# First token product of two batches by seven products, and five weight blocks rounded in attention: a fused attention and MLP-mixer kernel

## The chip, the core and the metric

The kernel runs on one core of one Trainium2 chip. The metric is the device time of one execution in microseconds (us). The core has a matrix engine (TensorE, PE in the profile; it loads weights as PEld and multiplies), a vector engine (VectorE, DVE), a scalar engine for activations and copies (ScalarE, ACT), GpSimd (POOL) and SyncE (SP), which here only issues transfers (DMA). Each engine works through its own list in order and waits on semaphores. Products land in PSUM[...].

## What is computed

Attention with a hash mask, on 4 batches, 8 heads, 768 tokens and 64 channels a head, feeds one MLP-mixer block: a product over the tokens, then one over the channels.

```python
def _attn_ref(q, k, v, proj):
    q_bits = (np.einsum('bhsd,dk->bhsk', q, proj) > 0)      # 6 bits, likewise k_bits
    ...
    mask = q_bucket[:, :, :, None] == k_bucket[:, :, None, :]
    scores = np.where(mask, scale * np.matmul(q, k.transpose(0, 1, 3, 2)), -1000000000.0)
    ...                                                      # softmax over the keys
    return np.matmul(attn, v)

def _moe_ref(x, w_tok1, w_tok2, w_ch1, w_ch2):               # x: 4 x 768 x 512
    xt = x.transpose(0, 2, 1)
    h = np.maximum(xt @ w_tok1, 0.0) @ w_tok2                # w_tok1 768x256, w_tok2 256x768
    u = x + h.transpose(0, 2, 1)
    h2 = np.maximum(u @ w_ch1, 0.0) @ w_ch2                  # w_ch1 512x1536, w_ch2 1536x512
    return (u + h2)
```

The four weights arrive in double precision. The kernel rounds them to single precision itself, from the two 32-bit words of each number, a block of 128 x 768 at a time.

## The kernel before

Attention goes through 16 pairs of heads, numbered 0 to 15; a pair is done in two halves of 384 queries. TensorE makes the scores (L337), ScalarE their exponentials `e` (L344), VectorE adds these up (`esd`, L371 to L378), TensorE weighs the values (L389) and sums over partitions (L413), VectorE refines the reciprocal (L426, L428) and divides (L438). Twelve blocks of weights are rounded meanwhile, one in each of pairs 0 to 11:

```python
# class Conversion, cut: steps of rounding one block
def fetch(self):
    ...
    raw = self.pool.tile([P, NW, 2], U32, name="raw", tag="raw", bufs=self.bufs)
    nc.sync.dma_start(out=raw..., in_=src)                                     # L169
def begin(self):
    size = self.pool.tile([P, NW], F32, name="size", tag="size", bufs=self.bufs - 1)
    nc.scalar.activation(size, raw[:, :, 1].bitcast(F32), ACT.Abs, scale=EXPONENTS)  # L177
def join(self):
    unit = self.pool.tile([P, NW], F32, name="unit", tag="unit", bufs=1)
    nc.vector.tensor_scalar(unit, size, 3, 0x7F800000, shift, and)             # L187
    nc.vector.tensor_scalar(size, size, 3, None, shift)                        # L191
    nc.vector.scalar_tensor_tensor(unit, raw[:, :, 0], 2.0**-52, unit, ...)    # L195
    nc.vector.tensor_tensor(size, size, unit, op=ALU.add)                      # L196
def end(self):
    nc.vector.scalar_tensor_tensor(to, hi, 0x80000000, size, and, or)          # L206
def turnover(self):
    self.end(); self.fetch()
def one(self):
    self.begin(); self.join(); self.end(); self.fetch()
```

```python
# attention's loop, cut
weights = Conversion(pool, [(w_tok1, W1, 3, (0, NR)), (w_tok2, W2, 1, (0, NJ)), (w_ch1, WC1, 1, (0, NCB))], bufs=2)
        for n in range(len(pairs)):
            halves = [Half(n, half) for half in range(2)]
            if n:
                load_v(n + 1)
            for now in halves:
                now.scores()
                if n == now.half == 0:
                    hashes(1)
                now.add()
                if now.half == 0:
                    now.add_last()
            if before:
                before.sums()
            if 0 < n < len(pairs) - 1:
                hashes(n + 1)
            halves[1].add_last()
            if n == 0:
                load_v(1)
            load_qk(n + 2)
            add_values(n)
            weights.begin()
            if before:
                before.newton()
            weights.join()
            halves[0].weigh()
            if n + 1 == len(pairs):
                before.divide()
                before = Quotients(halves)
                before.sums()
                before.newton()
                weights.turnover()
                halves[1].weigh()
                break
            if before:
                before.divide()
            weights.turnover()
            halves[1].weigh()
            if n and n % 2 == 0:
                bounce(pool.tile([P, 2 * S], F32, name="stage", tag="stage", bufs=1), n - 2)
            if n == 2 * NP:
                fetch(0, x0)
            before = Quotients(halves)
```

`bounce` turns two finished pairs of channels (two VectorE transposes, L233) and stores them to DRAM, from where the token stage fetches each batch as `x` with tokens on the partitions (L245).

In the token stage `mix1` makes the first product, 12 matmuls of 512 columns a batch (6 blocks of 128 tokens for each of 2 blocks of hidden units). `mix2` makes the second product by seven products in place of eight (Strassen's method in Winograd's form: sums of quarters on both sides beforehand, sums of the seven results after) and adds the result to XT in on-chip memory with an accumulating DMA. The eight blocks of the second channel weight (`conversion.one`) are rounded meanwhile, one `job` at a time.

```python
# tokens(), cut
        def mix1(b):
            x = (x0, x1)[b % 2]
            if b and turned:
                turn(b, x, banks)
            r1 = pool.tile([P, NJ, DM], F32, name="r1", tag="r1", bufs=2)
            for j in range(NJ):
                ps = bank("t1")
                for r in range(NR):
                    nc.tensor.matmul(
                        ps, W1[:, r, P * j : P * j + P], x[:, r], start=(r == 0), stop=(r == NR - 1),
                    )                                  # L634
                to = r1[:, j]
                if not turned:
                    to = to.rearrange("p (c g i) -> p g c i", c=NCB, i=32)
                    ps = ps.rearrange("p (g c i) -> p g c i", c=NCB, i=32)
                nc.scalar.activation(to, ps, ACT.Relu)
                job()
        ...
        def mix2(b, m):
            r1, new = R1[b]
            a00, a01, s1, a11 = (
                r1[:, k, P * (2 * m + i) : P * (2 * m + i) + P] for i in range(2) for k in range(2)
            )
            ...
            to = places[(2 * b + m + 1) % 3].rearrange("p (i n t) -> p i n t", i=2, n=2)
            p1, u, p7, p57 = (to[:, i, n] for i in range(2) for n in range(2))
            product(0, a00, b00)                       # product: one matmul, L674
            nc.scalar.copy(p1, ps[0])                  # L679
            product(1, a01, b10)
            product(2, s1, sums[:, 0])
            nc.scalar.copy(p57, ps[2])
            product(3, new[:, 1], b01)
            nc.scalar.copy(p7, ps[3])
            product(0, new[:, 0], sums[:, 1], False)
            nc.scalar.copy(u, ps[0])
            product(2, new[:, 2], b11, False)
            product(3, a11, sums[:, 2], False)
            ...                                        # five VectorE sums, L689 to L693
            nc.gpsimd.dma_start(out=XT[...], in_=to, accum_op=ALU.add)   # L694

        for b in range(B):
            mix1(b)
            if b == 0:
                weight_sums()
            left_sums(b)
            if b:
                mix2(b - 1, 0)
                job()
                mix2(b - 1, 1)
        mix2(B - 1, 0)
        inputs(0, T, 0)
        mix2(B - 1, 1)
        while not turned and jobs:
            job()
```

The channel stage follows (L761 is its matmul). It ends with a product whose four quarters go to the output as they are finished:

```python
# product(), cut
issuer = nc.scalar if j == 6 else nc.sync
...
issuer.dma_start(out=final(0, 0), in_=qs[:, 0])                       # L1173
...
issuer.dma_start(out=final(1, 1), in_=qs[:, 3])                       # L1180
...
for i, a in [(1, ps[2]), (2, ps[3])]:
    nc.vector.tensor_tensor(qs[:, i], a, qs[:, i], op=ALU.add)        # L1184
    issuer.dma_start(out=final(i // 2, i % 2), in_=qs[:, i])          # L1185
```

Of the kernel before, what the change touches and what calls it, by code (L numbers as in the profile page):

```python
# [35 lines left out]
F32 = mybir.dt.float32  # L37
# [11 lines left out]
def kernel(  # L49
# [14 lines left out]
    P = 128  # L64
# [76 lines left out]
    class Conversion:  # L141


        def __init__(self, pool, parts, bufs):
            self.pool, self.bufs = pool, bufs
            self.todo = [
                (w, dst, rows, j, n)
                for w, dst, rows, blocks in parts
                for j in range(*blocks, rows)
                for n in range(0, dst.shape[2], NW // rows)  # L150
            ]
            self.fetched, self.begun, self.ready = [], None, None
            for _ in range(bufs - 1):
                self.fetch()
# [17 lines left out]
        def begin(self):  # L172
            if not self.fetched:
                return
            raw, to, rows = self.fetched.pop(0)
            size = self.pool.tile([P, NW], F32, name="size", tag="size", bufs=self.bufs - 1)
            nc.scalar.activation(size, raw[:, :, 1].bitcast(F32), ACT.Abs, scale=EXPONENTS)  # L177
            self.begun = raw, size, to, rows

        def join(self):  # L180
            if not self.begun:
                return
            raw, size, to, rows = self.begun
            self.begun = None
            unit = self.pool.tile([P, NW], F32, name="unit", tag="unit", bufs=1)

            nc.vector.tensor_scalar(  # L187
                unit.bitcast(U32), size.bitcast(U32), 3, 0x7F800000,
                op0=ALU.logical_shift_left, op1=ALU.bitwise_and,
            )  # L190
            nc.vector.tensor_scalar(  # L191
                size.bitcast(U32), size.bitcast(U32), 3, None, op0=ALU.logical_shift_left,
            )

            nc.vector.scalar_tensor_tensor(unit, raw[:, :, 0], 2.0**-52, unit, op0=ALU.mult, op1=ALU.mult)  # L195
            nc.vector.tensor_tensor(size, size, unit, op=ALU.add)  # L196
            self.ready = raw, size, to, rows

        def end(self):

            if not self.ready:
                return
            raw, size, to, rows = self.ready
            self.ready = None
            hi, size = (a.rearrange("p (t n) -> p t n", t=rows) for a in (raw[:, :, 1], size.bitcast(U32)))
            nc.vector.scalar_tensor_tensor(  # L206
                to.bitcast(U32), hi, 0x80000000, size, op0=ALU.bitwise_and, op1=ALU.bitwise_or,
            )

# [15 lines left out]
    dram = ctx.enter_context(tc.tile_pool(name="dram", bufs=1, space=bass.MemoryType.DRAM))  # L225
    bounced = [dram.tile([S, DM], F32, name=f"bounced{b}") for b in range(B)]
# [31 lines left out]
    def attention(pool, psum, W1, W2, x0):  # L258
# [191 lines left out]
        for _ in range(12):  # L450
# [4 lines left out]
            [(w_tok1, W1, 3, (0, NR)), (w_tok2, W2, 1, (0, NJ)), (w_ch1, WC1, 1, (0, NCB))],  # L455
            bufs=2,
# [4 lines left out]
        for n in range(len(pairs)):  # L461
# [34 lines left out]
            weights.turnover()  # L496
            halves[1].weigh()
# [84 lines left out]
    def inputs(s, T, which):  # L582

        a, b = (slice(TT * (2 * s + i), TT * (2 * s + i) + TT) for i in range(2))
        low, high = slice(0, NCB // 2), slice(NCB // 2, NCB)
        if which == 0:
            nc.vector.tensor_tensor(T[0], XT[:, low, b], XT[:, low, a], op=ALU.subtract)
            nc.vector.tensor_tensor(T[2], XT[:, high, b], XT[:, low, b], op=ALU.subtract)
        else:
            nc.vector.tensor_tensor(T[1], XT[:, high, b], T[0], op=ALU.subtract)  # L590
            nc.vector.tensor_tensor(T[3], XT[:, high, a], T[1], op=ALU.subtract)

    def tokens(pool, psum, W1, W2, x0, weights, jobs, T, places):
# [7 lines left out]
        turned = not jobs  # L601
        if not turned:
            fetch(1, x1)
            jobs = jobs(weights(pool))
            bounce(places[2], len(pairs) - 2)
        NQ = DM // 2
        sums = pool.tile([P, 3, HALF], F32, name="W2sums", tag="W2sums", bufs=1)
        b00, b01, b10, b11 = (W2[:, k, HALF * n : HALF * n + HALF] for k in range(2) for n in range(2))

        def weight_sums():  # L610
            nc.vector.tensor_tensor(sums[:, 0], b01, b00, op=ALU.subtract)
# [4 lines left out]
        def job():  # L616
            if not turned and jobs:
                jobs.pop(0)()
# [6 lines left out]

        def mix1(b):
            x = (x0, x1)[b % 2]
            if b and turned:
                turn(b, x, banks)
            r1 = pool.tile([P, NJ, DM], F32, name="r1", tag="r1", bufs=2)  # L630
            for j in range(NJ):
                ps = bank("t1")
                for r in range(NR):
                    nc.tensor.matmul(  # L634
                        ps, W1[:, r, P * j : P * j + P], x[:, r], start=(r == 0), stop=(r == NR - 1),
                    )
                to = r1[:, j]
                if not turned:
                    to = to.rearrange("p (c g i) -> p g c i", c=NCB, i=32)
                    ps = ps.rearrange("p (g c i) -> p g c i", c=NCB, i=32)  # L640
                nc.scalar.activation(to, ps, ACT.Relu)
                job()
            if b % 2:
                new = pool.tile([P, 3, NQ], F32, name="r1s", tag="r1s", bufs=1)
            else:
                new = T[0].rearrange("p k t -> p (k t)")[:, : 3 * NQ].rearrange("p (i c) -> p i c", i=3)
            R1[b] = r1, new
            if not turned and b + 2 < B:
                fetch(b + 2, x)
# [12 lines left out]
        def mix2(b, m):  # L662
# [6 lines left out]
            ps = [bank("t2")[:, :HALF] for _ in range(4)]  # L669
            to = places[(2 * b + m + 1) % 3].rearrange("p (i n t) -> p i n t", i=2, n=2)  # L670
            p1, u, p7, p57 = (to[:, i, n] for i in range(2) for n in range(2))

            def product(at, left, right, start=True):
                nc.tensor.matmul(  # L674
                    ps[at], left, right, start=start, stop=True, skip_group_check=True,
                )

            product(0, a00, b00)
            nc.scalar.copy(p1, ps[0])  # L679
            product(1, a01, b10)  # L680
            product(2, s1, sums[:, 0])
            nc.scalar.copy(p57, ps[2])
            product(3, new[:, 1], b01)
            nc.scalar.copy(p7, ps[3])
            product(0, new[:, 0], sums[:, 1], False)
            nc.scalar.copy(u, ps[0])
            product(2, new[:, 2], b11, False)
            product(3, a11, sums[:, 2], False)
            nc.vector.tensor_tensor(p1, ps[1], p1, op=ALU.add)  # L689
            nc.vector.tensor_tensor(p57, p7, p57, op=ALU.add)  # L690
            nc.vector.tensor_tensor(p57, p57, u, op=ALU.add)  # L691
            nc.vector.tensor_tensor(p7, ps[3], u, op=ALU.add)
            nc.vector.tensor_tensor(u, ps[2], u, op=ALU.add)  # L693
# [4 lines left out]

        for b in range(B):
            mix1(b)  # L700
            if b == 0:
                weight_sums()
            left_sums(b)
            if b:
                mix2(b - 1, 0)
                job()
                mix2(b - 1, 1)
        mix2(B - 1, 0)
        inputs(0, T, 0)
        mix2(B - 1, 1)  # L710
        while not turned and jobs:
            job()
# [20 lines left out]
    def channels(pool, psum, SW1, second, TA, judge):  # L733
# [399 lines left out]
        def product(s, j, name, q, between, final=None):  # L1133
# [38 lines left out]
            if final:  # L1172
                issuer.dma_start(out=final(0, 0), in_=qs[:, 0])  # L1173
# [3 lines left out]
            if final:  # L1177
                nc.vector.tensor_tensor(qs[:, 3], qs[:, 3], u, op=ALU.add)
                nc.vector.tensor_tensor(qs[:, 3], qs[:, 3], p57[:, 0], op=ALU.add)
                issuer.dma_start(out=final(1, 1), in_=qs[:, 3])  # L1180
# [13 lines left out]
        def outputs(s):  # L1194
# [41 lines left out]
            if s < last:  # L1236
# [5 lines left out]
                    add(q2, q2, q1), store(q2, 0, 0), lambda: inputs(s + 1, T, 0), lambda: inputs(s + 1, T, 1),  # L1242
# [64 lines left out]
        inputs(0, T, 1)  # L1307
# [51 lines left out]
    def attention_and_tokens(W1, W2, x0):  # L1359
# [13 lines left out]
        def weights(pool):  # L1373
            return Conversion(pool, [(w_ch2, WC2, 3, (0, NHT))], bufs=3)

        def jobs(conversion):
# [3 lines left out]
            return [  # L1380
                lambda: (early(), late()),
                *[conversion.one] * (NHT * DM // NW),
            ]
# [3 lines left out]
        inside(tokens, W1, W2, x0, weights, jobs, [TA[:, 0], None, TA[:, 1], None], places)  # L1387

    def careful_attention_and_tokens(W1, W2, x0):
        def weights(pool, psum):  # L1390
            conversion = Conversion(pool, [(w_tok1, W1, 3, (0, NR)), (w_tok2, W2, 1, (0, NJ))], bufs=3)
# [10 lines left out]
        with tc.tile_pool(name="places", bufs=1, reuse_waits="tile") as pool:  # L1402
            places = [pool.tile([P, 2 * S], F32, name=f"place{i}") for i in range(3)]
            inside(tokens, W1, W2, x0, None, None, [TA[:, 0], None, TA[:, 1], None], places)
# [50 lines left out]
```

## Time and profile before

The time is 803.24 us, the median of three runs (802.8 to 804.15); the profiled execution spans 801.6 us. The stages, from the busy time of the engines in stretches of the span:

| stretch, us | what runs | PE busy | DVE busy | ACT busy | DMA share |
|---|---|---|---|---|---|
| 20 to 290 | attention, pairs 0 to 14 | 270.0 | 229.3 | 222.3 | 0.44 |
| 290 to 315 | attention's end | 25.0 | 17.4 | 19.0 | 0.43 |
| 315 to 334 | token stage, batches 0 and 1 | 19.0 | 16.4 | 5.8 | 0.81 |
| 334 to 375 | token stage, middle | 41.0 | 39.5 | 14.9 | 0.77 |
| 375 to 395 | token stage, end | 19.2 | 16.0 | 7.9 | 0.77 |
| 455 to 780 | channel stage | 325.0 | 272.9 | 142.8 | 0.63 |

DMA share is the mean busy share of the core's 16 transfer engines. A line of the profile in order of time (a group of like instructions) has the start in us, the busy time of the group in us, the engine, the line of the kernel, the operation, what it writes and reads, and how many; in brackets the idle time before it and what released it. An fp32 matmul is recorded as two. The wait lists give the engine and line that waited, what it waited for, the total in us, the number of times and the longest.

### The profile page before, as it was taken

To read this page: it belongs to the slowest core of one execution; us is meant where nothing else is said; L and a number is where in the kernel's file an instruction comes from. 1 tells how busy PE (TensorE), PEld (TensorE's weight loads), DVE (VectorE), ACT (ScalarE), POOL (GpSimd) and SP (SyncE) were. 2 spreads that over 40 slices of the span, in tenths; PEclk is the share of its full clock that TensorE was granted. 3 is DMA by queue.
4 is the path that set the end of the run, shared out by engine and by line. 5 is a ranking of instruction groups with operands and counts; after the bars stand their busy time and mean duration, and the time that the engine had idled before them with its cause. 6 is when DMAs were issued, how large, how long until landed. Compare 5 with 4: busy or idle time off the path is not lost.

```text
span 801.6 us, 10594 instructions
## 1 busy us (share of the span) xinstructions
PE 792.5 (99%) x3885; PEld 470.6 (59%) x3885; DVE 658.0 (82%) x881; ACT 441.6 (55%) x707; POOL 53.6 (7%) x77
## 2 busy tenths in 40 slices
PE   9999999999999999999999999999999999999996
PEld 5444444444444444455544458876667886666885
DVE  4889898989887677999677888988769897779986
ACT  5688888888888886333222221327773335775111
POOL 1000000000000000011121010011110012000010
PEclk9999999999999999999999999999999999999998
DMA  4435353537352424797636994599754577630455
GB/s 163 159 122 160 121 161 122 160 121 239 128 170 90 145 72 158 199 292 177 155 69 207 305 381 169 177 299 261 235 145 145 213 201 195 214 105 9 166 179 128
DMA packets 90972, 138.61 MB, mean 173 GB/s; under 512 B 29656, under 2 KB 63392, under 8 KB 88608
## 3 DMA queue, kind: packets, MB, share of 16 engines
q1 hardware_dynamic: 82192, 112.20, 42.2%
q0 software_dynamic: 7728, 24.64, 13.8%
q10 hardware_dynamic: 992, 1.00, 0.4%
q8 instruction: 33, 0.54, 0.3%
q14 instruction: 27, 0.22, 0.1%
HBM read 97.21 MB, written 33.16 MB: 163 GB/s over the span
## 4 chain that ended last, share of the span: by engine, by line
PE 95%; DVE 2%; DMA 1%; issue 0%; ACT 0%; DVEq 0%; ACTq 0%
PE b L761 50%; PE sc L337 20%; PE acc L389 16%; PE t L634 4%; PE t L674 2%; PE sums L413 2%; DMA XT<-second 1%; PE hp L298 1%; PE hw L316 0%; PE idle L451 0%; DVE size L196 0%; DVE unit L195 0%; DVE second L693 0%; DVE second L691 0%; DVE second L689 0%
## 5 line engine op out<-in xcount | busy, mean ns | idle before, releaser
L344 ACT ACTIVATE e<-sc 128x768 f32<-128x768 f32 x192 | 154.0, 811 | 12.4 <-PE sc L337 12.0
L337 PE MATMUL sc<-qk 64*128 64x384 f32 x768 | 156.7, 487 | 0.0
L761 PE MATMUL b<-R,second 128*128 128x256 f32 (+1 forms) x612 | 150.9, 404 | 0.0
L761 PEld LDWEIGHTS b<-R,second 128*128 128x128 f32 x612 | 116.3, 190 | 31.6 <-issue 17.2
L767 ACT COPY c<-b 128x512 f32<-128x512 f32 (+1 forms) x78 | 37.5, 488 | 169.1 <-PE b L761 158.5
L389 PE MATMUL acc<-e,vn 128*64 128x384 f32 x768 | 127.6, 488 | 0.0
L375 DVE TENSOR_TENSOR esd<-esd,e 128x768 f32<-128x768 f32 x96 | 92.0, 958 | 10.0
L389 PEld LDWEIGHTS acc<-e,vn 128*64 128x64 f32 x768 | 53.6, 137 | 73.1 <-issue 71.1
L337 PEld LDWEIGHTS sc<-qk 64*128 64x128 f32 x768 | 67.5, 187 | 49.1 <-issue 47.6
L761 PE MATMUL b<-XT,WC 128*128 128x256 f32 (+1 forms) x264 | 82.5, 456 | 0.0
L761 PEld LDWEIGHTS b<-XT,WC 128*128 128x128 f32 x264 | 50.2, 190 | 29.6 <-issue 24.9
L337 PE MATMUL sc<-bits 64*128 64x384 bf16 x384 | 62.9, 323 | 0.2 <-DVE bits L320 0.2
L371 DVE SCALAR_TENSOR_TENSOR esd<-e 128x768 f32<-128x768 f32 x32 | 30.6, 955 | 28.1 <-ACT e L344 28.1
L634 PE MATMUL t<-x,W 128*128 128x512 f32 x96 | 41.8, 593 | 0.0
L395 ACT ACTIVATE num<-acc,vsum 128x384 f32<-128x384 f32 x32 | 18.6, 581 | 31.7 <-PE acc L389 31.3
L694 POOL DMA_DIRECT2D XT<-second x8 | 9.9, 1232 | 391.8 <-DVE second L693 365.9
L434 ACT COPY rec<-rec 32x384 f32<-32x384 f32 x64 | 32.6, 510 | 5.0 <-DVE rec L428 4.2
L761 PE MATMUL b<-XT,SW 128*128 128x256 f32 (+1 forms) x120 | 34.6, 422 | 0.0
L337 PEld LDWEIGHTS <-bits 64*128 64x128 bf16 x384 | 19.3, 94 | 25.4 <-DVE bits L320 0.8
L761 PE MATMUL b<-TA,WC 128*128 128x512 f32 x72 | 33.8, 592 | 0.0
L761 PE MATMUL b<-TA,SW 128*128 128x512 f32 x72 | 32.9, 592 | 0.0
L378 DVE TENSOR_TENSOR esd<-esd,e 128x768 f32<-128x768 f32 x32 | 30.5, 954 | 1.9
(214 smaller groups left out, 1131.5 us busy)
## 6 DMA issues: line engine op xcount, KB each, us to landing
second<-left SPq DMA_DIRECT2D x18, 1344.0 KB
raw<-in_moe_w_ch SPq DMA_DIRECT2D x16, 768.0 KB
qk<-in_qk SPq DMA_DIRECT2D x15, 768.0 KB
seen<-in_qk POOLq DMA_DIRECT2D x21, 384.0 KB, 4.1
WC<-hidden_left SPq DMA_DIRECT2D x15, 448.0 KB
vn<-in_v SPq DMA_DIRECT2D x16, 384.0 KB
vt<-in_vT SPq DMA_DIRECT2D x16, 384.0 KB
x<-bounced SPq DMA_DIRECT2D x4, 1536.0 KB
```

Of the source, the lines that this page charges most:

```text
L337: nc.tensor.matmul(sc[:, i, :HALF], t[rows, 1, P * c : P * c + P], t[rows, 0, qs], start=start, stop=not start,)
L344: nc.scalar.activation(e, sc[:, :, :HALF], ACT.Exp, scale=SCALE)
L371: nc.vector.scalar_tensor_tensor(self.d, es[0], NR * EPS, es[1], op0=ALU.add, op1=ALU.add,)
L375: nc.vector.tensor_tensor(self.d, self.d, e, op=ALU.add)
L378: nc.vector.tensor_tensor(self.d, self.d, self.es[-1], op=ALU.add)
L389: nc.tensor.matmul(acc[D * i : D * i + D], vn[:, i, c], e[:, i], start=(c == 0), stop=(c == NR - 1),)
L395: nc.scalar.activation(nums[self.n][:, self.half], acc, ACT.Identity, scale=-1.0, bias=vsum,)
L413: nc.tensor.matmul(ps[at : at + 32], ones[:, :32], self.halves[h].d[:, i], start=True, stop=True,)
L434: nc.scalar.copy(rec[other : other + 32, h], rec[at : at + 32, h])
L634: nc.tensor.matmul(ps, W1[:, r, P * j : P * j + P], x[:, r], start=(r == 0), stop=(r == NR - 1),)
L761: nc.tensor.matmul(ps, left(k), right(k), start=start and k == ks[0], stop=stop and k == ks[-1], skip_group_check=True,)
L767: nc.scalar.copy(c, ps)
```

## The change

The first token product of batches 2 and 3 is made by seven products too: each product is then 3 matmuls of 256 columns, 21 in place of 12 of 512. This needs sums of W1's quarters once (`left`), sums of x's quarters for each of the two batches (`right_sums`), and five sums of the results before the relu. To make room on VectorE in the token stage, five of the eight blocks of the second channel weight are rounded during attention's last pairs, 12 to 15, which had none; their place is not free yet then, so the rounded block is written into `unit` and from there to DRAM (`wc2`), and the five are fetched back in the token stage at batch 2. Pair 14 rounds two. The sums of the first channel weight move from the stage's start to its second half. Two of the last four output stores are issued by SyncE and no longer by ScalarE.

```diff
# Conversion
+            away = to.space == bass.MemoryType.DRAM
             nc.vector.scalar_tensor_tensor(
-                to.bitcast(U32), hi, 0x80000000, size, op0=ALU.bitwise_and, op1=ALU.bitwise_or,
+                (unit if away else to).bitcast(U32), hi, 0x80000000, size,
+                op0=ALU.bitwise_and, op1=ALU.bitwise_or,
             )
+            if away:
+                nc.sync.dma_start(out=to, in_=unit)
...
+    wc2 = dram.tile([P, NHT, DM], F32, name="wc2")
...
# attention
-            [(w_tok1, W1, 3, (0, NR)), (w_tok2, W2, 1, (0, NJ)), (w_ch1, WC1, 1, (0, NCB))],
-            bufs=2,
+            [
+                (w_tok1, W1, 3, (0, NR)), (w_tok2, W2, 1, (0, NJ)), (w_ch1, WC1, 1, (0, NCB)),
+                (w_ch2, wc2, 3, (0, NHT)),
+            ],
+            bufs=2, which=slice(len(pairs) + 1),
...
             weights.turnover()
+            if n == 12:
+                weights.fetch()
+            if n == 14:
+                weights.one()
             halves[1].weigh()
...
# token stage
+        def right_sums(b):
+            x00, x01, x10, x11 = quarters(b)
+            nc.vector.tensor_tensor(right[:, 0], x01, x00, op=ALU.subtract)
+            nc.vector.tensor_tensor(right[:, 1], x11, right[:, 0], op=ALU.subtract)
+            nc.vector.tensor_tensor(x01, x11, x01, op=ALU.subtract)
+            nc.vector.tensor_tensor(right[:, 2], x10, right[:, 1], op=ALU.subtract)
...
+            seven([bank("t1")[:, :NQ] for _ in range(4)], to, [
+                (u00, x00), (u01, x10), (s1, t1), (s3, x01), (s2, t2), (s4, x11), (u11, t4),
+            ])
...
+        if not turned:
+            bounce(places[2], len(pairs) - 2)
+            jobs.pop("start")()
+        weight_sums()
         for b in range(B):
...
             mix1(b)
-            if b == 0:
-                weight_sums()
+            if not turned:
+                if b + 2 < B:
+                    fetch(b + 2, (x0, x1)[b % 2])
+                if b == 2:
+                    for k, c in [(slice(0, 6), slice(0, DM)), (slice(6, 9), slice(0, DM // 2))]:
+                        nc.sync.dma_start(out=second["WC2"][:, k, c], in_=wc2[:, k, c])
+                if 0 < b < B - 1:
+                    right_sums(b + 1)
+                for job in jobs.pop((b, "middle"), []):
+                    job()
+            if b:
+                mix2(b - 1, 0)
+            if b > 1:
+                relus(b)
             left_sums(b)
             if b:
-                mix2(b - 1, 0)
-                job()
                 mix2(b - 1, 1)
+            if not turned:
+                for job in jobs.pop((b, "end"), []):
+                    job()
...
+            return {
+                "start": one, (0, "end"): [one], (1, "end"): [one], (2, "end"): [early],
+                (3, "middle"): [late],
+            }
...
# last product
-                issuer.dma_start(out=final(0, 0), in_=qs[:, 0])
+                nc.sync.dma_start(out=final(0, 0), in_=qs[:, 0])
...
-                issuer.dma_start(out=final(1, 1), in_=qs[:, 3])
+                nc.sync.dma_start(out=final(1, 1), in_=qs[:, 3])
```

`seven` is the body of `mix2` with several matmuls to a product (L664 of the changed kernel); the sums over partitions are L424 there.

## The prediction

> **What bounds the kernel now.** I read the page's busy times and chain first, then who waited for whom on TensorE, then the stretches that the change touches, in order of time.
>
> ```profile
> PE 792.5 (99%) x3885; PEld 470.6 (59%) x3885; DVE 658.0 (82%) x881; ACT 441.6 (55%) x707; POOL 53.6 (7%) x77
> ...
> PE 95%; DVE 2%; DMA 1%; issue 0%; ACT 0%; DVEq 0%; ACTq 0%
> ```
>
> TensorE (PE) is busy 99% of the span and is 95% of the chain that ended last. Its waits name everything it lost between start and tail:
>
> ```profile
> PE idle L451 <- DVE ones L97: 1.0, 1, 1.0
> PE t L674 <- ACT second L679: 0.8, 1, 0.8
> PE sc L337 <- DVE bits L320: 0.2, 1, 0.2
> ```
>
> Hence only two things count: TensorE columns taken away, and any wait put where there is none now. TensorE's order of time around the end of attention and in the token stage:
>
> ```profile
> 306.40 4.09 PE L389 MATMUL acc<-e,vn 128*64 128x384 f32 x24
> 310.43 0.85 PE L413 MATMUL sums<-esd,ones 128*32 128x384 f32 x8
> 311.21 4.09 PE L389 MATMUL acc<-e,vn 128*64 128x384 f32 x24
> 315.23 20.87 PE L634 MATMUL t<-x,W 128*128 128x512 f32 x48
> ...
> 344.96 10.46 PE L634 MATMUL t<-x,W 128*128 128x512 f32 x24
> ```
>
> The reader is to see that nothing stands between the attention pairs, and that one batch of the first token product (24 records, two per fp32 product, so 12 products of 512 columns) takes 10.3 us, from 344.96 to the next start at 355.26. VectorE (DVE) at the same place, last two pairs of attention:
>
> ```profile
> 293.09 0.96 DVE L438 TENSOR_TENSOR XT<-num,rec 128x768 f32<-128x768 f32 x1 [1.67 <-ACT rec L434]
> 293.96 1.83 DVE L233 STREAM_TRANSPOSE stage<-XT 128x768 f32<-128x768 f32 x2
> 298.50 0.96 DVE L371 SCALAR_TENSOR_TENSOR esd<-e 128x768 f32<-128x768 f32 x1 [2.70 <-ACT e L344]
> ...
> 307.87 0.96 DVE L378 TENSOR_TENSOR esd<-esd,e 128x768 f32<-128x768 f32 x1
> 308.75 0.55 DVE L426 TENSOR_TENSOR t<-sums,near 128x384 f32<-128x384 f32 x1
> ```
>
> The sums of pair 15 (298.50 to 308.83) end only 1.6 us before the TensorE product that needs them (L413 at 310.43). That product also needs t of pair 14 (L426), which frees its PSUM bank at 309.30: 1.1 us of slack. A rounding of one weight block, in pair 11 which still has one:
>
> ```profile
> 233.74 0.56 DVE L187 TENSOR_SCALAR unit<-size 128x768 uint32<-128x768 uint32 x1
> 234.33 0.56 DVE L191 TENSOR_SCALAR size<-size 128x768 uint32<-128x768 uint32 x1
> 234.81 0.95 DVE L195 SCALAR_TENSOR_TENSOR unit<-raw,unit 128x768 f32<-128x768 uint32 x1
> 235.79 0.96 DVE L196 TENSOR_TENSOR size<-size,unit 128x768 f32<-128x768 f32 x1
> ```
>
> With its last step (0.96 us) a rounding is 3.9 us of VectorE when it stands alone.
>
> **What the Trainium skill says.** "DMA: Bandwidth & Descriptors", section "Anatomy of one DMA", gives a fixed 2.0 us plus bytes over 436 GB/s, mostly the receipt from the target memory. The trace agrees: a 786 KB store (left<-seen), issued at 421.40, held VectorE until 424.73, and one issued at 427.92 until 431.93: 3.3 and 4.0 us against 3.8. A stored block here is 393 KB, estimated 2.9 us from that page. The same page, "Issuing engines are not separate DMA queues", says that another issuing engine saves only issue time; that is all the moved last stores can bring. "VectorE: DVE Perf Modes", section "The DRAIN you can't avoid", says that the next operation waits until the pipe is empty. The trace agrees for chained sums: they start 1.06 us apart (three in 3.08), unchained ones 0.88. So a late chain doesn't catch up.
>
> **The change part by part.**
>
> *Fewer columns.* A 256-column fp32 product costs 0.43 us: later in this trace six records of that shape take 1.29 us, from 480.05 to 481.34. Seven products over three row blocks are 21 of them, 9.0 us against 10.3. Two batches: -2.5 us. Batches 0 and 1 become 24 products of 256 columns, 10.3 us, as now.
>
> *VectorE in the token stage.* Five roundings leave: -19.6 us. Sums of W1 (4 x 0.5), of two x (8 x 1.0) and of the seven products (10 x 0.43) come: +14.3 at most. None is on the path as long as it stays ahead of TensorE, which I laid out below.
>
> *Roundings in attention.* Pairs 12, 13 and 15 get one each. VectorE is busy 12.1 to 13.9 us of 19 in these windows and 17.5 in pair 10, with a rounding and a bounce; these fit. Pair 14 gets two and a bounce, and here is a wait. The rounded block goes through `unit`, of which there is one buffer, to DRAM; the second rounding's first step writes `unit`, so it waits for that store to land. The order of the built program shows this semaphore. Step by step: rec of pair 13 ends at 291.4; rounding A with the division of L438 inside ends at 296.15 (pair 11's 238.5, moved by 57.6 us); the store is issued at 296.2, after the eight bit copies that end at 295.6; with 2.9 us it lands at about 299.1; rounding B ends its turn at 303.0 and the bounce's two transposes at 304.8. The sums of pair 15 start there and not at 298.5: 6.3 us late, and as a chain they stay so. L426 ends at 315.6 and not 309.3, so TensorE's L413 starts at about 315.7. ScalarE costs a little too: the second `size` also has one buffer, so its 0.92 us stands before pair 14's numerator and pair 15's exponentials, which start 0.75 us late; the score banks give back part, and TensorE loses 0.4 us early in pair 15. L413 would then be free to go at 310.8 and waits some 4.9 us. Together +5.3.
>
> *Start of the token stage.* SyncE now issues the last store, a raw block and x of batch 1 in a row behind the end of pair 15's rounding, which the chain above puts at 323.0 (315.6, two rec 1.0, four steps 3.0, division 0.9, t and rec 1.5, last step 1.0). They carry 0.39 + 0.79 + 1.57 = 2.75 MB. The same two loads moved at 400 GB/s between 309 and 313.5 in the trace; with the start-up and receipt x lands at about 331.8. TensorE finishes batch 0 at 315.8 + 4.8 + 10.35 = 330.95. +0.8 us.
>
> *Later token stage.* Carried on like this VectorE has the W2 sums at 336.5 (wanted at 342), the x sums of batch 2 at 346 (351), those of batch 3 at 365 (369), and stays just ahead at the end. The old 0.84 us wait hung on the accumulating DMA of three half-batches earlier (issued at 381.30, landed at 391.1). That DMA is now issued about 0.7 us later relative to TensorE, because half of the WC1 sums stands before it, but the residual stores and the copy that it shared the queues with are over earlier. I put -0.8 for the old wait and +0.3 for a new one.
>
> *Tail.* In the last product ScalarE issued four stores, one of which took 1.63 us (793.96), so the last two went out at 795.68 to 796.9 although their data was ready at 794.9 and 795.3. Two now go by SyncE, whose issue takes 0.34 us: -0.8.
>
> Sum: 803.2 - 2.5 - 0.8 - 0.8 + 5.3 + 0.8 + 0.3 = 805.5 us.
>
> **The rivals.** *A: pair 14 hides its two roundings.* Then only the arithmetic counts: 803.2 - 2.5 - 0.8 - 0.8, perhaps +0.3, so 799.4. For it speaks that pair 14 leaves VectorE 5 us idle now, and that someone chose this pair with care; against it the one `unit` and the 1.1 us of slack. *B: VectorE or a transfer becomes the bound in the token stage.* It was busy 39.5 of 41 us between 334 and 375, and x, raw blocks and wc2 share one queue. If x of batch 1 comes 2 us later, and the last half-batches wait 2 us for their place, the time is 808.5. Against it speaks the net -5 us of VectorE. *C: the stall is real but TensorE makes part of it good*, because the old idle places move behind it. For that the chain of waits has too little idle, 0.8 us: at most 804.7.
>
> **Range and chances.** The stall of pair 14 is the term that decides: 4 to 6 us as the store takes 2 to 4, and near 0 if I misread the order, which I give 1 in 8. The rest is ±1.5. That makes 805.5 with 801.5 to 808.5. Two per cent is 16 us, far out of reach of any of these terms either way.
>
> **What would show it.** Right: L424 (the sums product) of pair 15 waits about 5 us on VectorE, the first esd of pair 15 starts 6 us late, VectorE waits about 3 us for the store wc2<-unit; each seven-product batch of L664 takes 9.0 us; the token stage's first product of batch 1 waits for x. Wrong: a time below 801, with pair 15's sums on time; or VectorE waits inside the token stage of more than 3 us, which would put it above 808.

## The result, and the profile after

The changed kernel takes 807.73 us, the median of six runs (807.54 to 809.13); the kernel before took 803.19 us beside it (802.65 to 804.15). The ratio is 1.0059 with a 95% interval of 1.0046 to 1.0072: some 4.5 us slower. The profiled executions span 805.6 and 801.6 us.

The page of the changed kernel, busy times and chain:

```profile
PE 793.0 (98%) x3969; PEld 487.1 (60%) x3969; DVE 670.1 (83%) x903; ACT 444.5 (55%) x719; POOL 53.5 (7%) x77
...
PE 94%; DVE 3%; ACT 1%; issue 1%; DMA 0%; DVEq 0%
```

TensorE's busy time has not fallen (792.5 before), although it does less work, and VectorE is 3% of the chain that ended last (2% before). The waits of TensorE:

```profile
PE sums L424 <- DVE t L437: 4.9, 1, 4.9
PE idle L462 <- DVE ones L98: 1.0, 1, 1.0
PE sc L348 <- DVE bits L331: 0.2, 1, 0.2
```

One wait is new, the one on VectorE at pair 15's sums; the 0.8 us wait at the end of the token stage is gone. TensorE in order of time, from pair 15's sums to the first seven-product batch:

```profile
316.38 1.51 PE L424 MATMUL sums<-esd,ones 128*32 128x384 f32 x8 [4.88 <-DVE t L437]
317.82 5.41 PE L400 MATMUL acc<-e,vn 128*64 128x384 f32 x24
323.17 21.05 PE L706 MATMUL t<-x,W 128*128 128x256 f32 x96
...
353.08 2.75 PE L664 MATMUL t<-x,W 128*128 128x256 f32 x12
...
362.14 1.45 PE L664 MATMUL t<-W,r 128*128 128x384 f32 x4
```

The seven-product batch goes from 353.08 to 362.14: 9.06 us. But the line of the sums shows two things, not one: the idle time, and then 1.51 us for eight records that took 0.85 before; the weighing after it takes 5.41 us where it took 4.09. From the first sum to the token stage there are 6.79 us (316.38 to 323.17) instead of 4.80. The view by stretches says why; its columns are the stretch and its length, the busy time of PE, PEld, DVE, ACT and POOL, the clock granted to TensorE as a part of full speed, the share of the transfer engines, and GB/s:

```profile
311.50:316.40 4.90, 0.02 (x3) 0.02 (x3) 4.45 (x7) 0.00 (x0) 0.00 (x0) 0.73 0.00 0
316.40:317.80 1.40, 1.40 (x8) 0.18 (x8) 1.40 (x3) 0.83 (x2) 0.00 (x0) 0.50 0.00 0
317.80:320.00 2.20, 2.20 (x12) 0.97 (x10) 2.13 (x4) 2.15 (x5) 0.00 (x0) 0.50 0.00 0
320.00:323.20 3.20, 3.20 (x21) 1.10 (x17) 3.17 (x6) 1.45 (x4) 0.00 (x0) 0.92 0.00 0
```

During the idle time the clock falls to one half, and it stays there when the work begins again. VectorE, which TensorE waited for:

```profile
295.94 0.95 DVE L213 SCALAR_TENSOR_TENSOR unit<-raw,size 128x768 uint32<-128x768 uint32 x1
299.89 0.56 DVE L191 TENSOR_SCALAR unit<-size 128x768 uint32<-128x768 uint32 x1 [2.99 <-DMA wc<-unit]
...
305.57 0.92 DVE L382 SCALAR_TENSOR_TENSOR esd<-e 128x768 f32<-128x768 f32 x1
...
315.78 0.55 DVE L437 TENSOR_TENSOR t<-sums,near 128x384 f32<-128x384 f32 x1
```

The second rounding of pair 14 waits 2.99 us for the store of the first; behind it come the rounding itself, the bounce and, at 305.57, pair 15's first sum. Before, that sum began at 298.50.

By stages, after less before, from the two profiles: start to the end of pair 14's weighing +1.0 (of which 0.8 lies in the very first products; the profiled executions of the kernels here differ there by up to 3.3 us without any change to that code, the first sums over partitions beginning between 36.52 in run 1 and 39.80 in run 6), the wait +4.9, the slower sums and weighing of pair 15 +2.0, token stage -3.4 (75.13 us against 78.53), channel stage 0.0, from the last group of products to the end -0.5 (10.59 against 11.12). That makes +4.0, the difference of the spans.

### The profile page after: what moved, and what is told of

Read it like the earlier page. It is cut to its first block, busy times and chain, and to the rows that moved or that the text cites. A ratio compares the mean times of both kernels' runs of the same rounds, so it can differ in the third digit from the quotient of the medians.

```text
span 805.6 us, 10813 instructions
## 1 busy us (share of the span) xinstructions
PE 793.0 (98%) x3969; PEld 487.1 (60%) x3969; DVE 670.1 (83%) x903; ACT 444.5 (55%) x719; POOL 53.5 (7%) x77
## 4 chain that ended last, share of the span: by engine, by line
PE 94%; DVE 3%; ACT 1%; issue 1%; DMA 0%; DVEq 0%
PE b L849 50%; PE sc L348 17%; PE acc L400 14%; PE t L664 7%; PE t L706 3%; PE sums L424 1%; PE hp L309 1%; ACT e L355 1%; DVE esd L386 1%; PE hw L327 1%; DMA wc<-unit 0%; PE idle L462 0%; DVE esd L389 0%; DVE size L200 0%; DVE stage L244 0%
## 5 line engine op out<-in xcount | busy, mean ns | idle before, releaser
L849 PEld LDWEIGHTS b<-XT,SW 128*128 128x128 f32 x120 | 22.8, 190 | 10.8 <-issue 7.0
```

The lines of the kernel that those rows point to most:

```text
L849: nc.tensor.matmul(ps, left(k), right(k), start=start and k == ks[0], stop=stop and k == ks[-1], skip_group_check=True,)
```

## The experiments

The theory: a late VectorE in pair 14 costs the 4.9 us wait, its idle time costs 2.0 us more through the clock, and the seven products are worth their columns, 2.5 us. Rivals: the slow products after the wait come from something other than the idle time; the store is not what makes VectorE late; or VectorE's sums eat what the seven products save. All times are medians, and ratios are to the kernel before, with 95% intervals.

**1. Fill the idle time.** TensorE gets seven products, whose result nobody reads, where it idled. They need only data that is there already.

```diff
                 before = Quotients(halves)
+                fill = psum.tile([P, 2, 512], F32, name="fill", tag="sc", bufs=3)
+                for _ in range(7):
+                    nc.tensor.matmul(fill[:, 0, :HALF], halves[0].es[0][:, 0, :P], halves[0].es[0][:, 1], ...)
                 before.sums()
```

> The changed kernel with seven more fp32 products (128 x 128 x 384, results never read) put on TensorE just ahead of pair 15's sums over partitions, where it stands idle for 4.9 us; 7 x 0.64 = 4.5 us of work, nothing else changed. Theory (the idle time also lowers TensorE's granted clock, and the work after it runs at half speed for some 4 us): the sums still start at about 316.4 on the trace, but they and the weighing after them take 4.8 us as in the kernel before and not 6.8, the granted clock stays 1.00, and the time falls by 2.0 us to about 805.7. Rival (the slow products after the wait are slow because their inputs come late, not because of the clock): the same time as the changed kernel within 0.3 us, or longer.

Measured: 808.15 us, ratio 1.0062 (1.0050 to 1.0074). TensorE in this kernel's order of time:

```profile
315.34 0.85 PE L424 MATMUL sums<-esd,ones 128*32 128x384 f32 x8
316.12 4.09 PE L400 MATMUL acc<-e,vn 128*64 128x384 f32 x24
320.66 2.86 PE L711 MATMUL t<-x,W 128*128 128x256 f32 x12 [0.45 <-DVE t L437]
323.96 8.04 PE L711 MATMUL t<-x,W 128*128 128x256 f32 x36 [0.44 <-ACT num L406]
333.45 10.63 PE L711 MATMUL t<-x,W 128*128 128x256 f32 x48 [1.45 <-DMA x<-bounced]
```

The sums and the weighing have their old 0.85 and 4.09 us, at a granted clock of 1.00 from 306 to 325: the slow products came from the idle time. But the total has not moved. The 2.0 us won came back as three waits, 0.45 + 0.44 + 1.45 = 2.3 us, the largest for x of batch 1, which was issued at 323.57 and released TensorE at 333.45. From the end of pair 14's weighing to the channel stage the profile has 87.7 us, against 86.9 in the changed kernel. The mechanism is shown; that it sets the time of the changed kernel is not, until x is out of the way (run 9).

**2. Take away the wait for the store.** Pair 14's first rounded block goes to the tile `stage` and from there to DRAM, so that `unit` is free at once. (A second buffer of `unit` was not tried.)

```diff
+            if n == 14:
+                weights.end(pool.tile([P, 2 * S], F32, name="stage", tag="stage", bufs=1)[:, :NW])   # unit = stage
             weights.turnover()
```

> The changed kernel with one thing altered: pair 14's first rounded block is written into the bounce's stage tile, not into unit, and stored from there, so the second rounding needn't wait for that store. Theory (the single unit makes 3.0 of the 6.3 us that VectorE is late): the second rounding now waits only for its size step on ScalarE, begins at 297.9 and not 299.9, pair 15's sums begin 2.0 us earlier and TensorE's wait falls from 4.9 to 2.9 us; the time falls by 2 us, by up to 4 if the shorter idle time spares the clock. Rival (two roundings and a bounce are simply too much VectorE work for this pair, the store hardly matters): TensorE's wait stays above 4.3 us and the time within 0.6 us of the changed kernel's.

Measured: 805.70 us, ratio 1.0030 (1.0018 to 1.0042), 2.0 us less than the changed kernel. VectorE and TensorE of this kernel:

```profile
297.94 0.56 DVE L191 TENSOR_SCALAR unit<-size 128x768 uint32<-128x768 uint32 x1 [0.97 <-ACT size L181]
```

```profile
314.43 1.00 PE L426 MATMUL sums<-esd,ones 128*32 128x384 f32 x8 [2.85 <-DVE t L439]
```

The store's share is 2.0 us of the 4.9; the remaining 2.9 us of wait are the second rounding itself, with its 0.97 us wait for ScalarE's size step. The clock falls here too: 6.44 us from the first sum to the token stage, against 4.80 undisturbed.

```profile
314.40:316.00 1.60, 1.57 (x10) 0.45 (x12) 1.56 (x4) 0.99 (x2) 0.00 (x0) 0.69 0.00 0
316.00:318.00 2.00, 2.00 (x10) 0.72 (x8) 1.97 (x3) 1.95 (x5) 0.00 (x0) 0.50 0.00 0
318.00:321.00 3.00, 3.00 (x19) 1.17 (x16) 2.96 (x6) 1.25 (x4) 0.00 (x0) 0.93 0.00 0
```

One short wait is new, 0.47 us on ScalarE at batch 1.

**3. Round four blocks in attention, not five.** Pair 14 rounds one; the fifth goes back to the token stage.

```diff
-            if n == 12:
-                weights.fetch()
-            if n == 14:
-                weights.one()
...
-            bufs=2, which=slice(len(pairs) + 1),
+            bufs=2, which=slice(len(pairs)),
...
-                "start": one, (0, "end"): [one], (1, "end"): [one], (2, "end"): [early],
+                "start": lambda: (early(), one()), (0, "end"): [one], (1, "end"): [one], (2, "end"): [one],
```

> The changed kernel with four blocks rounded in attention, one in each of pairs 12 to 15, and four in the token stage; pair 14 has no second rounding. The first half of the WC1 sums moves to the stage's start, the fourth rounding takes its place after batch 2. Theory (pair 14's second rounding makes the whole loss, the token stage gains what was worked out): no wait before pair 15's sums, no fall of the clock, the token stage takes 75.2 us, time 807.7 - 4.9 - 2.0 - 0.2 = 800.6, faster than the kernel before by 2.5 us. Rival (the room made in the token stage is needed, VectorE is the bound there with four roundings): TensorE waits 3 us or more inside the token stage, and the time is 803 or more.

Measured: 801.37 us, ratio 0.9977 (0.9968 to 0.9986), 6.4 us less than the changed kernel. The sums no longer wait, and the 4.80 us from them to the token stage are back. One wait appeared that the long one had covered, at batch 1:

```profile
313.30 0.85 PE L424 MATMUL sums<-esd,ones 128*32 128x384 f32 x8
...
318.10 10.63 PE L702 MATMUL t<-x,W 128*128 128x256 f32 x48
329.69 10.60 PE L702 MATMUL t<-x,W 128*128 128x256 f32 x48 [0.96 <-DMA x<-bounced]
```

**4. The moved stores alone.** In the kernel before, only the two stores go by SyncE.

```diff
-                issuer.dma_start(out=final(0, 0), in_=qs[:, 0])
+                nc.sync.dma_start(out=final(0, 0), in_=qs[:, 0])
...
-                issuer.dma_start(out=final(1, 1), in_=qs[:, 3])
+                nc.sync.dma_start(out=final(1, 1), in_=qs[:, 3])
```

> The kernel before with only the two output stores of the last product moved from ScalarE to SyncE. Theory (ScalarE's issue of four stores in a row delayed the last two): the last store is issued about 0.8 us earlier after TensorE's end and the time falls by 0.5 us, to about 802.7. Rival (the end is set by the landing of the last bytes and the end of the program, not by the issue): the same time within 0.2 us.

Measured: 803.20 us, ratio 0.9995 (0.9986 to 1.0004). The profile shows 10.57 us from the last group of products to the end, 11.12 before, so -0.55; the interval of the time holds both that and nothing.

**5 and 6. Fetch x first.** On run 3's kernel, x of batch 1 is fetched ahead of the raw block (5); then the same with eight products in every batch, so without the sums of x, of W1 and of the results (6).

```diff
+            fetch(1, x1)
             jobs = jobs(pool)
-            fetch(1, x1)
```

> The kernel of the four-block run with one transfer moved: x of batch 1 is asked for ahead of the raw block and not behind it. Theory (in that run TensorE waited 1.0 us for x because the stored block and 0.79 MB of raw data went ahead of it in the queue): the wait for x is gone, x landing some 2 us earlier, the token stage takes 75.2 us, and the time falls by 1.0 us to about 800.4. Rival (VectorE now gets its raw block too late and the W2 sums or the roundings hold up TensorE): a wait of 1 us or more appears further on and the time stays at 801.4 or above.

> The kernel of the run above with the seven products of batches 2 and 3 taken out again: all four batches by 24 products of 256 columns, without the sums of W1, of x and of the seven results; the roundings stay where they are. Theory (the seven products are worth their TensorE columns and nothing else): batch 2's and batch 3's first product take 10.3 us and not 9.0, the time is 2.5 us longer than that run's, about 802.9. Rival (moving the roundings was the gain, the seven products' sums eat what they save): within 0.8 us of that run.

Measured: 805.27 us (ratio 1.0026, 1.0016 to 1.0036) and 807.61 us (1.0061, 1.0035 to 1.0088). Run 5 went against the theory: x is there on time, but the raw block is late instead and VectorE with it: its first rounding begins 12.6 us after the token stage's first product, 8.9 in run 3. That line, and the longest of TensorE's waits that are not in run 3:

```profile
328.04 0.56 DVE L191 TENSOR_SCALAR unit<-size 128x768 uint32<-128x768 uint32 x1 [3.63 <-ACT size L181]
...
PE b L845 <- DVE second L679: 2.2, 1, 2.2
```

VectorE did not make up what it lost at the stage's start; TensorE pays at its end, with these 2.2 us and 1.1 more on ScalarE (0.2 on ScalarE came earlier). Run 6 is 2.3 us above run 5, as the columns say, but it has waits of its own there (2.6 and 0.6 us), so it doesn't decide. Run 10 repeats it without them.

**7. Fill, and x first.** Runs 1 and 5 together, on the changed kernel.

> The changed kernel with seven filling products ahead of pair 15's sums, as in the first run, and x of batch 1 asked for ahead of the raw block. Theory (the filling gave back the clock's 2.0 us, but TensorE then came to batch 1 before its x had landed, a second wait hidden behind the first): no wait for x, the clock stays 1.00, and the time is 2.0 us below the changed kernel's, near 805.7. Rival (the filled time is lost otherwise, for instance to the products' own inputs): near 808 as in the first run.

Measured: 812.95 us, ratio 1.0114 (1.0089 to 1.0139). The theory failed as in run 5: 4.8 us of new waits in the token stage, 4.1 of them at its end (2.6 on ScalarE, of which 0.8 earlier, and 2.2 on VectorE).

**8. x in two halves.** Run 3's kernel, the order of the transfers as it was, but x of batch 1 fetched as two halves of 256 columns. The first product of the batch then needs only the first half.

```diff
             jobs = jobs(pool)
-            fetch(1, x1)
+            for c in range(2):
+                half = slice(DM // 2 * c, DM // 2 * c + DM // 2)
+                nc.sync.dma_start(out=x1[:, :, half], in_=bounced[1].rearrange(...)[:, :, half])
```

> The kernel of the four-block run (raw block ahead of x, as it was) with x of batch 1 asked for in two halves of 256 columns, so that the first products of batch 1 need only 0.79 MB of it. Theory (in that run TensorE waited 1.0 us for x, and VectorE has just enough room if its raw block isn't put back): the wait for x is gone, no new one comes, and the time falls by about 1.0 us to 800.4. Rival (VectorE's chain of roundings and sums is as tight as x, as the run with x first showed): the wait moves to the end of the token stage, and the time stays within 0.4 us of 801.4.

Measured: 799.95 us (798.8 to 801.1), ratio 0.9959 (0.9946 to 0.9973): faster than both kernels. TensorE's waits in it, all of them:

```profile
PE hw L327 <- DMA qk<-in_qk: 1.3, 1, 1.3
PE idle L462 <- DVE ones L98: 1.0, 1, 1.0
PE sc L348 <- DVE bits L331: 0.2, 1, 0.2
```

Nothing waits behind the start of the kernel. The token stage takes 75.07 us.

**9. Fill, and x in two halves**, on the changed kernel.

> The changed kernel with the seven filling products ahead of pair 15's sums, and x of batch 1 in two halves behind the raw block. Theory (behind the stall x of batch 1 is the next wait, so only with both is the clock's 2.0 us gained, less 0.9 us for two new short waits on PSUM banks that the first run's trace shows): no wait for x, clock 1.00, about 806.6. Rival (after the stall VectorE is the next wait whatever x does): 807.7 or more, with TensorE's new waits on VectorE or ScalarE in the token stage.

Measured: 806.26 us, ratio 1.0042 (1.0028 to 1.0055), 1.5 us less than the changed kernel. The clock keeps its speed (-2.0), x is no longer waited for, and the waits of 0.45 and 0.44 us of run 1 are left (+0.9): -1.1 by this sum, and -0.9 (86.0 us for 86.9) in the profile from the end of pair 14's weighing to the channel stage. The slow clock is no peculiarity of one profiled execution: the mean clock over the whole kernel is 0.993 to 0.996 in the six timed executions of the changed kernel, and 0.997 to 0.999 in the five of this one. What x in two halves alone would do for the changed kernel was not run.

**10. Eight products on the best kernel.** Run 8 with eight products in batches 2 and 3 and without their sums.

```diff
-            if b < 2:
+            if True:
                 for j in ...                     # eight products
-            nc.vector.tensor_tensor(left[:, 3], w10, w11, op=ALU.add)     # and three more, of W1
-                if 0 < b < B - 1:
-                    right_sums(b + 1)
-            if b > 1:
-                relus(b)
```

> The same kernel as the one with four blocks in attention and x of batch 1 in two halves (799.95 us), but with eight products in the last two batches, so without the sums of x and of the weight quarters. Theory: on a base in which no other wait ends this stage, each seven-product batch is worth exactly its missing columns, 1.25 us, so 2.5 us in all: about 802.4 us, and each of the two batches takes about 10.3 us from its first product to the next batch's instead of 9.06. Rival: VectorE's sums take as much as they save by delaying what follows, so the time stays within 0.8 us of 799.95.

Measured: 802.98 us (801.12 to 805.21), ratio 0.9995 (0.9983 to 1.0007), 3.0 us above run 8. The rival's 0.8 us is out. Each of the two batches takes 10.36 us (345.40 to 355.76, and 364.79 to 375.15) and took 9.07 in run 8: 2.6 us for both. One wait is back, the one of the kernel before that the change had removed:

```profile
PE t L658 <- ACT second L663: 1.0, 1, 1.0
```

ScalarE waits there for an accumulating DMA, issued at 383.25 and landed at 391.86: 8.6 us. In run 8 it was 7.6 us (381.79 to 389.37), and TensorE did not feel it.

## Why the prediction was right, point by point

The prediction was 805.5 us with 801.5 to 808.5, the time is 807.73. The mechanism is the one predicted; the sum left out one term of 2 us, and two small terms were counted that the trace doesn't show. These two, +0.8 and +0.3, made up for half of the missing one, so that the sum came as near as it did is partly luck.

*Store and second rounding, right.* Predicted: the store issued at 296.2 lands at 299.1, pair 15's sums begin 6.3 us late, t ends at 315.6. The 2.9 us for the store was an estimate from "DMA: Bandwidth & Descriptors", section "Anatomy of one DMA", in the Trainium skill, which describes transfers issued by GpSimd; this one is SyncE's, and the trace bears the figure out all the same: issued at 296.92, landed at 299.89 (3.0 us), sums begin at 305.57, 7.1 us later than before, of which 0.8 is the chance difference at the start, and t ends at 316.3. The wait was put at 4.9 us and is 4.88. Run 2 splits it: 2.0 for the store, 2.9 for the rounding. ScalarE's extra 0.4 us was 0.2.

*After the wait, wrong.* The prediction let TensorE go on at 315.7 and reach the token stage "at 315.8 + 4.8". It took 6.79 us and not 4.8, because the clock stood at one half. "TensorE: Matmul & The Clock Gate" in the Trainium skill says it in its section "Part 1: The HAM clock gate": the gate passes one half of the clock after an idle window of about 3.4 us, and all of it after as long a busy one; the window runs freely. I hadn't applied it. The traces agree on how long the slow clock lasts. A mean of 0.73 over 4.90 us is 46% of it at full clock and the rest at one half, which puts the fall at 313.75; the 0.92 puts the rise at 320.5: 6.8 us, two windows. In run 2 the same working, from the means of 0.69 and 0.93, gives 315.0 and 318.4: 3.4 us, one window. They do not agree that a whole window must be idle. The clock fell when TensorE had been idle for 2.3 us, and in run 2 an idle time of 2.85 us was enough, the fall coming after the work had begun again. The slow clock was the missing +2.0.

*Seven products, right.* 9.06 us a batch against a predicted 9.0, and run 10 shows 2.6 us for the two. Rival B, VectorE as the bound in the token stage, did not occur in the changed kernel; run 5 shows that it does when VectorE is late by 3.7 us. Rival C did not occur either: the old wait of 0.8 us is gone in run 8 too, where there is no stall, so the stall did not buy it back.

*x of batch 1, +0.8, not seen.* The wait was named as a sign of being right, and it did not show. TensorE came to batch 1 about 2.6 us later than I had laid out (0.8 of it from the start), and x was there. The term was real beneath it: with the stall or the slow clock gone it appears as 0.96 us in run 3 and 1.45 in run 1. Its size was about right; that the clock would cover it was not foreseen.

*The old wait, -0.8, right*, and no new one in its place (+0.3 predicted, 0 measured): 3.4 us less in the token stage are 2.5 for the columns and 1.1 for the wait (0.84 us idle and a slower start after it), less 0.2 that batches 0 and 1 take longer with 256 columns. Run 10 shows how near that wait still is.

*Tail, -0.8*: the profiles of the change and of run 4 show -0.5, and the timed runs cannot tell it from nothing.

Put together from the profile: -2.5 - 1.1 + 0.2 - 0.5 + 4.9 + 0.2 + 2.0 = +3.2, and +4.0 with the chance difference at the start; timed, it is +4.5 (3.7 to 5.8). Of the 1.3 us between, about 0.3 lie outside the span (the time exceeds it by 1.8 us in the kernel before and by 2.1 in the changed one); about one microsecond is not assigned to a cause.

Rival A, 799.4 us, was wrong for this kernel but right as arithmetic: with the stall taken away by the four blocks and x in halves, run 8 has 799.95.

## What to carry to other kernels

A product that saves columns is worth just its columns if the work that makes room for it is put where its engine has time; here one rounding too many in one pair cost more than twice what both batches saved. Ask of a TensorE wait whether it must be counted twice: once as idle time and once for the slow clock after it, 1.6 us after 2.85 us of waiting and 2.0 us after 4.9 here. A wait that goes away uncovers the next one, so take the margins of what follows from the trace before adding up a gain, and before changing the order of transfers on one queue, ask what the one put back is needed for.

## What was not expected of the hardware

- TensorE's clock fell 2.3 us into an idle time of 4.9 us and came back 4.1 us after the work had begun again. An idle time of 2.85 us was followed by a fall as well, 0.6 us after the restart, which cost 1.6 us.
- The length of a wait alone does not tell whether the clock will fall. Waits of 2.25 us (runs 5 and 7) and 2.35 us (run 6) at the end of the token stage left it at 1.00; a wait of 1.80 us near the start of run 3 was followed by half clock from about 11.1 to 14.5 us, 1.1 us after the work had begun again.
- Seven products that nobody needs, 4.86 us of work in an idle time of 4.9 us, kept the clock at 1.00; together with x in two halves they brought 1.5 us (run 9), and without it nothing (run 1).
- x of 1.57 MB, behind 0.39 and 0.79 MB on its queue, released TensorE 9.9 us after its issue (323.57 to 333.45, run 1), with the last bounce's stores issued beside it from 326.80; in halves of 0.79 MB it held nobody up (run 8).
